# W2's block sums and split halves, made once and read back from DRAM, in a Strassen feed-forward kernel

## The chip, the cores and the metric

The kernel runs on one core of one Trainium2 chip. The metric is device time in microseconds (us), the median of several executions; smaller is better. The core's engines work side by side, each through its own queue in order: TensorE (PE in the profile; PEld is its weight load), VectorE (DVE), ScalarE (ACT), GpSimd (POOL) and SyncE (SP), which here only issues DMAs.

## The reference

Sliding-window attention with four sink tokens is followed by a Fourier mixing layer and a feed-forward block. The part that matters here is the end:

```python
u = x + mixed                               # x: attention output, 4 x 768 tokens x 512
mu = np.mean(u, axis=-1, keepdims=True)
var = np.mean((u - mu) ** 2, axis=-1, keepdims=True)
un = (u - mu) / np.sqrt(var + 1e-06)
ch = np.maximum(un @ w_ch1, 0.0) @ w_ch2    # w_ch1: 512 x 2048, w_ch2: 2048 x 512
return (u + ch).astype(np.float32)
```

All data is float32. TensorE multiplies in a rounded float32 (fp32r), so each operand is kept as a rounded high part and a low part, the rest, and a product is three matmuls: high x high, high x low, low x high.

## The kernel before

**Stages.** Attention and the Fourier mixing of the four batches come first; their code is not touched. The 3072 tokens are then taken through the feed-forward block in six groups of 512. Group 0 runs in a plain form while the weights are still being converted (`convert`, L595 and around), with W2 multiplied as it is. Groups 1 to 5 use a Strassen form of the second matmul; they are one loop (`for g in range(1, len(groups))`, L1391 on) that writes out the order of every engine's work by hand (`manual_schedule`), so each engine does its work exactly in the order of the code.

**A step.** Inside a group the loop over `q` runs eight times; this text calls one pass a step. A step handles 256 of the 2048 hidden columns, as two chunks of 128. `ch1` (matmuls on L629) multiplies the first chunk: 12 matmuls of 512 columns into one PSUM bank, `h0`. ScalarE's relu (L1396) moves it to the SBUF tile `r4`. Then TensorE does the first half of the products of the step before (`slot(prev, slice(0, 7))`, L1292, 21 matmuls of 256 columns), then `ch1` of the second chunk, whose relu is L1413, then the other half of the products (`slot(prev, slice(7, 14))`, 21 more). So TensorE alternates 12 + 21 + 12 + 21 matmuls a step. Because both `ch1` of a step write the same bank, the next `ch1` has to wait until the relu has emptied it; and that relu has to wait until VectorE has read the old contents of `r4`.

**The Strassen operands.** The left ones come from the hidden activations: `first_h`, `second_h` and `third_h` make four sums on VectorE (L1252, L1258, L1260, L1261) and split seven blocks into halves, the high one a ScalarE copy (L1247), the low one a VectorE subtraction (L1248): per step two of 256 columns, one of 512, one of 768. The right ones come from W2: `w_sums` makes four sums of 256 columns (L1272 to L1275) and `split_w` splits seven blocks in five pieces, the high halves on ScalarE (L1283), the low ones (L1284) on GpSimd, except for two pieces a step that VectorE does in the last group. W2 is the same for every group, but these sums and halves are made anew in each of the 40 steps, since only one set of them has room: the tiles `WC` (in the profile `w_ring`, `w2t`) are overwritten as soon as the products of the step before have read them.

**Work laid between.** `prepare(g + 1)` normalizes the next group's tokens in small pieces, taken by `next(steps, None)`: statistics (L507, L508), an inverse root by fourteen tiny operations (L514 to L523), the normalization (L531), sixteen 32 x 32-block transposes for each token block (`turn_blocks`, L1154), and the split of the result into `un_slots` or `un_last` (L541 ScalarE, L546 VectorE). Before, each step takes three pieces after its first half, one ahead of `third_h` and two behind it, so all is done by the seventh step. At the start of a group the seven accumulators of the group before are added into `u` (`finish_a`, `finish_b`, `finish_c`, L1314, VectorE), then three additions of SBUF to SBUF follow on GpSimd (`finish_d`, also L1314), and SP stores the result (L1349). `reload` (L1148) brings blocks of the other batches from DRAM into the freed places.

## Time and profile before

| | |
|---|---|
| median of 3 runs | 848.51 us (848.25 to 849.68) |
| profiled execution, its own time | 850.29 us |
| its span, first to last instruction | 848.5 us |
| VectorE busy | 714.5 us (84%) |
| ScalarE busy | 409.2 us (48%) |
| GpSimd busy | 543.2 us (64%) |
| bytes moved by DMA | 57.85 MB |

Engines overlap, so the shares add to more than the span. The five Strassen groups begin at 337.8, 437.4, 542.3, 645.8 and 750.7 us of the span, by the start of each group's first relu (L1396). A row of the trace gives start, duration, engine, line, operation and, in brackets, how long the engine had been idle before and for whom it waited. A row of a group gives busy time and mean duration in ns, and one of a single line minimum, median and maximum in ns. PEclk, in a row of windows, is the clock that TensorE was granted, 1.00 being full speed.

### The profile page before, as it was taken

To read this page: it belongs to the slowest core of one execution; us is meant where nothing else is said; L and a number is where in the kernel's file an instruction comes from. 1 tells how busy PE (TensorE), PEld (TensorE's weight loads), DVE (VectorE), ACT (ScalarE), POOL (GpSimd) and SP (SyncE) were. 2 spreads that over 40 slices of the span, in tenths; PEclk is the share of its full clock that TensorE was granted. 3 is DMA by queue.
4 is the path that set the end of the run, shared out by engine and by line. 5 is a ranking of instruction groups with operands and counts; after the bars stand their busy time and mean duration, and the time that the engine had idled before them with its cause. 6 is when DMAs were issued, how large, how long until landed. Compare 5 with 4: busy or idle time off the path is not lost.

```text
span 848.5 us, 14292 instructions
## 1 busy us (share of the span) xinstructions
PE 766.2 (90%) x4899; PEld 641.7 (76%) x4899; DVE 714.5 (84%) x1636; ACT 409.2 (48%) x1053; POOL 543.2 (64%) x644
## 2 busy tenths in 40 slices
PE   7989989989899999898897979979789788899994
PEld 5667767767788787787796867968679677799993
DVE  6786687897999995898889988899889997898765
ACT  5776665766332233353453434534445344455551
POOL 3465484585654454566596765968669585687762
PEclk9999999999989999989999989989999998999998
DMA  9835236333134560200000020000200000000001
GB/s 322 254 101 172 61 83 210 91 114 102 48 124 150 198 215 10 100 1 1 0 1 25 1 75 1 1 25 3 74 1 1 26 25 1 2 1 26 25 2 55
DMA packets 41827, 57.85 MB, mean 68 GB/s; under 512 B 2796, under 2 KB 27500, under 8 KB 41360
## 3 DMA queue, kind: packets, MB, share of 16 engines
q1 hardware_dynamic: 41456, 53.07, 19.7%
q0 software_dynamic: 288, 3.76, 1.1%
q8 instruction: 41, 0.67, 0.3%
q14 instruction: 42, 0.34, 0.1%
HBM read 47.37 MB, written 9.45 MB: 67 GB/s over the span
## 4 chain that ended last, share of the span: by engine, by line
PE 59%; DVE 28%; issue 6%; ACT 4%; POOL 2%; DMA 1%; SPq 0%; ACTq 0%; DVEq 0%; POOLq 0%
PE h L629 23%; PE p L1292 12%; DVE unf L1154 6%; PE o L1130 5%; DVE h_sums L1248 5%; PE xt L799 4%; PE s L712 4%; PE za L387 2%; PE pt L761 2%; DVE sums L1260 2%; DVE u L1314 1%; PE zb L387 1%; DVE sums L1258 1%; DVE f L344 1%; DVE un L531 1%
## 5 line engine op out<-in xcount | busy, mean ns | idle before, releaser
L1247 ACT CAST h_sums<-sums 128x256 fp32r<-128x256 f32 (+2 forms) x160 | 90.7, 567 | 185.1 <-DVE sums L1261 113.0
L1248 DVE TENSOR_TENSOR h_sums<-sums,h_sums 128x256 fp32r<-128x256 f32 (+2 forms) x160 | 137.8, 869 | 15.3 <-ACT h_sums L1247 9.9
L1292 PE MATMUL p<-w_ring,h_sums 128*128 128x256 f32 x960 | 136.3, 284 | 14.0 <-DVE h_sums L1248 8.8
L1292 PEld LDWEIGHTS p<-w_ring,h_sums 128*128 128x128 f32 x960 | 126.6, 191 | 18.7 <-DVE h_sums L1248 9.9
L1284 POOL TENSOR_TENSOR w2t<-sums,w2t 128x256 fp32r<-128x256 f32 x72 | 59.6, 828 | 112.2 <-ACT w2t L1283 111.8
L629 PE MATMUL h<-un_slots,w 128*128 128x512 f32 x396 | 108.6, 428 | 16.4 <-ACT sums L1396 16.2
L629 PE MATMUL h<-un_last,w 128*128 128x512 f32 x396 | 104.2, 415 | 18.1 <-ACT sums L1396 14.7
L1292 PE MATMUL p<-w2t,h_sums 128*128 128x256 f32 x720 | 112.5, 283 | 0.0
L629 PEld LDWEIGHTS h<-un_slots,w 128*128 128x128 f32 x396 | 80.5, 208 | 34.9 <-ACT sums L1396 17.4
L629 PEld LDWEIGHTS h<-un_last,w 128*128 128x128 f32 x396 | 77.5, 202 | 35.5 <-ACT sums L1396 16.1
L1292 PEld LDWEIGHTS p<-w2t,h_sums 128*128 128x128 f32 x720 | 101.0, 192 | 3.5
L736 ACT ACTIVATE sm<-sm,mx 128x132 f32<-128x132 f32 x192 | 75.9, 399 | 14.4 <-DVE mx L730 14.4
L1154 DVE STREAM_TRANSPOSE unf<-un 32x128 f32<-32x128 f32 x256 | 77.5, 303 | 4.2
L712 PE MATMUL s<-ring,q 64*128 64x260 f32 x320 | 55.6, 430 | 7.9 <-DVE mx L730 7.8
L1284 POOL TENSOR_TENSOR w_ring<-sums,w_ring 128x512 fp32r<-128x512 f32 x32 | 46.0, 1437 | 12.4 <-ACT w_ring L1283 11.7
L1284 POOL TENSOR_TENSOR w_ring<-w2r,w_ring 128x512 fp32r<-128x512 f32 x40 | 53.2, 1330 | 0.5 <-ACT w_ring L1283 0.5
L1258 DVE TENSOR_TENSOR sums<-sums 128x256 f32<-128x256 f32 x40 | 30.6, 766 | 26.7 <-ACT sums L1413 26.4
L747 POOL CAST sk<-sm 128x32 fp32r<-128x32 f32 x48 | 11.7, 244 | 64.6 <-ACT sm L736 64.6
L1284 POOL TENSOR_TENSOR w2t<-w2r,w2t 128x256 fp32r<-128x256 f32 x40 | 37.5, 938 | 20.0 <-ACT w2t L1283 20.0
L730 DVE CUSTOM_DVE_ANT_0 sm<-s,mask 128x132 f32<-128x132 f32 x192 | 47.5, 284 | 3.3 <-PE s L710 1.4
L718 DVE COPY_PREDICATED s<-older,s 128x256 f32<-128x256 uint8 x80 | 33.7, 422 | 16.7 <-PE s L712 16.4
L1413 ACT ACTIVATE sums<-h 128x512 f32<-128x512 f32 x40 | 23.8, 596 | 40.5 <-PE h L629 40.3
(235 smaller groups left out, 1770.0 us busy)
## 6 DMA issues: line engine op xcount, KB each, us to landing
raw<-in_moe_w_ch_dram SPq DMA_DIRECT2D x32, 512.0 KB, 3.3
ldv<-in_v_dram SPq DMA_DIRECT2D x28, 256.0 KB, 2.8
ring<-in_qk_dram SPq DMA_DIRECT2D x24, 264.0 KB, 5.0
out_dram<-u SPq DMA_DIRECT2D x24, 256.0 KB, 2.3
q<-in_qk_dram SPq DMA_DIRECT2D x20, 256.0 KB, 4.6
cst<-in_dft_dram POOLq DMA_DIRECT2D x1, 3348.0 KB, 12.7
ud<-us SPq DMA_DIRECT2D x12, 256.0 KB, 2.1
u<-ud SPq DMA_DIRECT2D x2, 1024.0 KB, 5.1
```

The source lines that it names most:

```text
L629: T.matmul(ps[:, :tb], a[:, cs], x[:, :, cc, :], start=n == 0, stop=n == 3 * NCC - 1)
L712: T.matmul(ps[:, j, :P + W], st["q", g][rows, hp, :], keys(g, 2 * hp + j), start=True, stop=True)
L730: V.tensor_tensor_reduce(sm[:, h % 4], ps[:, j, P:P + W], mask[min(qi, 3)], -SCALE, 3.0e38, ALU.add, ALU.min, accum_out=mx[:, 0, h:h + 1])
L736: A.activation(sm[:, h % 4], sm[:, h % 4], AF.Exp, bias=mx[:, 0, h:h + 1], scale=-1.0, accum_out=mx[:, 1, h:h + 1])
L799: T.matmul(ps[D * j:D * j + D, p, :], st["v", kb(g) - i][:, h, :], a[:, h % 4, :], start=i == 0, stop=i == n - 1)
L1130: T.matmul(po[i], a[:, ts_], x, start=f == 0 and n == 0, stop=f == NF - 1 and n == 2)
L1154: V.transpose(unf[32 * q:32 * q + 32, :, r], un[r].rearrange("p (c q j) -> p c q j", c=NCC, q=4)[:, :, q])
L1247: A.copy(hc_hi[:, left(a, n)], src)
L1248: V.tensor_tensor(hc_lo[:, left(a, n)], src, f32(hc_hi[:, left(a, n)]), op=ALU.subtract)
L1258: V.tensor_tensor(hs4[:, 1], r4[:, 0, 1], r4[:, 1, 1], op=ALU.add)
L1284: eng.tensor_tensor(lo, src, f32(hi), op=ALU.subtract)
L1292: T.matmul(acc[i][:, 2 * P * tp:2 * P * tp + 2 * P], x, w, start=q == 0 and tp == 0 and n == 0, stop=q == NF // 2 - 1 and n == 2, skip_gro ...
```

## The change

In group 1 the four sums and the low halves of W2's pieces are made on VectorE, and each finished piece is stored to a DRAM tile of its step (`w_dram`, `w2s` in the order below). In groups 2 to 5 `w_sums` and `split_w` are gone: five loads per step (`load_w2`, on SP's queue) bring both halves of each piece straight into the tiles. The three additions of `finish_d` move from GpSimd to VectorE; those of the last group's ending (`finish_last`) stay. The next group's blocks are, while group 1 runs, transposed by TensorE in the bank `h0` (`un_turn`), in the middle of the first half of the products; in groups 2 to 4 VectorE goes on transposing. The pieces of `prepare` are spread by two tables over all eight steps, `second_h` makes its sums before its split, `reload` comes two steps later, and group 0's outputs are finished in two portions.

```diff
+PREP_A = (0, 1, 1, 1, 1, 1, 1, 1), (0, 2, 2, 3, 3, 3, 3, 2)
+PREP_B = (1, 1, 1, 0, 0, 0, 0, 0), (1, 2, 2, 2, 2, 2, 2, 1)
-RELOAD_AT = 4
+RELOAD_AT = 6
+PARTS_W = (0, 0, 2, 0), (1, 0, 1, 2), (1, 1, 1, 3), (2, 0, 2, 4), (3, 0, 1, 6)
+    w_dram = [dpool.tile([P, 2, len(LEFT) * 2 * P], F32, name=f"w2s{q}") for q in range(NF // 2)]
...
                     un_make(b, blk, u)
                     yield
+                    if g == 2:
+                        turns.append((b, blk, unT, i))
+                        while turns:
+                            yield
+                        continue
...
-                split_h(r4[:, 1].rearrange("p t w -> p (t w)"), 2, 2)
                 V.tensor_tensor(hs4[:, 2], hs4[:, 1], r4[:, 0, 0], op=ALU.subtract)
                 V.tensor_tensor(hs4[:, 3], r4[:, 1, 0], hs4[:, 2], op=ALU.subtract)
+                split_h(r4[:, 1].rearrange("p t w -> p (t w)"), 2, 2)
...
-                G.tensor_tensor(t3, b22, b12, op=ALU.subtract)
+                V.tensor_tensor(t3, b22, b12, op=ALU.subtract)
...
+            def load_w2(q, i):
+
+                c, k, n, at_ = PARTS_W[i]
+                nc.sync.dma_start(f32(WC[c][:, :, 2 * P * k:2 * P * (k + n)]), w_dram[q][:, :, 2 * P * at_:2 * P * (at_ + n)])
...
                 A.copy(hi, src)
-                eng.tensor_tensor(lo, src, f32(hi), op=ALU.subtract)
+                V.tensor_tensor(lo, src, f32(hi), op=ALU.subtract)
+                nc.sync.dma_start(w_dram[q][:, :, 2 * P * at_:2 * P * (at_ + n)], f32(t))
...
-                    add(G, x, state["u2"])
+                    add(V, x, state["u2"])
...
-                        slot(prev, slice(0, 7))
+                        slot(prev, slice(0, 3))
+                        turned = turns.pop() if turns else None
+                        if turned:
+                            un_turn(*turned[:2], state["h"].tile([P, 512], F32, tag="h0", name=f"unt_{g + 1}_{turned[3]}"))
+                            un_hi(*turned)
+                            un_lo(*turned)
+                        slot(prev, slice(3, 7))
                         first_h()
...
+                            if prev[0] == 1 and prev[2]:
+                                split_w(prev[2], 3)
+                                split_w(prev[2], 4)
...
-                            w_sums(q)
-                            split_w(q, 1)
-                            split_w(q, 0)
-                        for _ in range(3):
+                            if g == 1:
+                                w_sums(q)
+                            else:
+                                load_w2(q, 1)
+                                load_w2(q, 0)
...
+                        for _ in range(PREP_A[g > 1][q]):
                             next(steps, None)
...
                         second_h()
+                        if g > 1:
+                            for i in range(2, 5):
+                                load_w2(q, i)
+                        elif q:
+                            for i in (1, 0, 2):
+                                split_w(q, i)
...
-                        for _ in range(2):
+                        for _ in range(PREP_B[g > 1][q]):
                             next(steps, None)
```

The first place is VectorE in the middle of group 1, one step (`sums` are the operand sums, `un`/`unf` the normalized block and its transpose). Before:

```order
L1252 TENSOR_TENSOR sums_4176<-sums_4175 128x256
L1248 TENSOR_TENSOR h_sums<-sums_4175,h_sums 128x256
L1248 TENSOR_TENSOR h_sums<-sums_4176,h_sums 128x256
L531 TENSOR_SCALAR un_3_4549<-u_65,stat_2_4259 128x512
L1154 STREAM_TRANSPOSE unf_1_4551<-un_3_4549 32x4x32 x8
L1258 TENSOR_TENSOR sums_4176<-sums_4175 128x256
L1248 TENSOR_TENSOR h_sums<-sums_4175,h_sums 128x512
L1260 TENSOR_TENSOR sums_4176<-sums_4176,sums_4175 128x256
L1261 TENSOR_TENSOR sums_4176<-sums_4175,sums_4176 128x256
L1154 STREAM_TRANSPOSE unf_1_4551<-un_3_4549 32x4x32 x4
L1248 TENSOR_TENSOR h_sums<-sums_4176,h_sums 128x768
L1154 STREAM_TRANSPOSE unf_1_4551<-un_3_4549 32x4x32 x4
```

And of the change, from the split of the previous step's last two pieces on, to the split of the next ones:

```order
L1298 TENSOR_TENSOR w_ring<-sums_4184,w_ring 128x512
L1298 TENSOR_TENSOR w2t_3956<-w2r_3554,w2t_3956 128x256
L1280 TENSOR_TENSOR sums_4184<-w2r_3722 128x256
L1281 TENSOR_TENSOR sums_4184<-w2r_3722 128x256
L1282 TENSOR_TENSOR sums_4184<-w2r_3722,sums_4184 128x256
L1283 TENSOR_TENSOR sums_4184<-w2r_3722,sums_4184 128x256
L534 TENSOR_SCALAR un_3_4656<-u_65,stat_2_4265 128x512
L1266 TENSOR_TENSOR sums_4183<-sums_4182 128x256
L1267 TENSOR_TENSOR sums_4183<-sums_4183,sums_4182 128x256
L1268 TENSOR_TENSOR sums_4183<-sums_4182,sums_4183 128x256
L1256 TENSOR_TENSOR h_sums<-sums_4182,h_sums 128x512
L1298 TENSOR_TENSOR w2t_3304<-sums_4184,w2t_3304 128x256
```

Nine operations on W2 stand in VectorE's row where none stood, and the sixteen transposes of a block are gone from it.

The second place is VectorE in group 2, from the sums of the second half of its second step (`u_1` is the part of the accumulators that three blocks share). Before:

```order
L1258 TENSOR_TENSOR sums_4176<-sums_4175 128x256
L1248 TENSOR_TENSOR h_sums<-sums_4175,h_sums 128x512
L1260 TENSOR_TENSOR sums_4176<-sums_4176,sums_4175 128x256
L1261 TENSOR_TENSOR sums_4176<-sums_4175,sums_4176 128x256
L519 SCALAR_TENSOR_TENSOR stat_0_5153<-stat_0_5153 128x4
```

And of the change:

```order
L1266 TENSOR_TENSOR sums_4183<-sums_4182 128x256
L1267 TENSOR_TENSOR sums_4183<-sums_4183,sums_4182 128x256
L1268 TENSOR_TENSOR sums_4183<-sums_4182,sums_4183 128x256
L1256 TENSOR_TENSOR h_sums<-sums_4182,h_sums 128x512
L1329 TENSOR_TENSOR u_64<-u_64,u_1_5084 128x2x256
L517 TENSOR_SCALAR stat_0_5143<-stat_0_5143 128x4
```

One of GpSimd's three additions a group has come in, and the inverse root begins here instead of in the half before.

The third place is SP's queue in group 2 (`w2s` is the DRAM copy, `ud` a batch kept in DRAM). Before, these rows follow each other, the last already of group 3:

```order
L1349 DMA out_dram<-u_64 128x512 x2
L1349 DMA out_dram<-u_65 128x512 x2
L1148 DMA u_64<-ud_66 128x1024
L1148 DMA u_65<-ud_67 128x1024
L1349 DMA out_dram<-u_65 128x512 x4
```

With the change, from the same stores on:

```order
L1364 DMA out_dram<-u_64 128x512 x2
L1364 DMA out_dram<-u_65 128x512 x2
L1288 DMA w2t_3304<-w2s_73 128x2x256
L1288 DMA w_ring<-w2s_73 128x2x512
L1288 DMA w2t_3304<-w2s_73 128x2x256
L1288 DMA w_ring<-w2s_73 128x2x512
L1288 DMA w2t_3956<-w2s_73 128x2x256
L1288 DMA w2t_3304<-w2s_74 128x2x256
```

Five loads a step, 256, 512, 256, 512 and 256 KB, stand in one queue with the stores and reloads.

More of the change, by code (lines that the diff above doesn't have):

```diff
@@ L603, in convert @@
                     if which:
-                        state["w2t", f] = d
+                        state["w2t", f] = state["ring"][:, 2 * i:2 * i + 2]
                 elif which:
                     if f == 2:
-                        state["w2t", f] = [pool.tile([P, 512], F32R, name=f"w2t{f}_{j}") for j in range(2)]
-                    d = state["w2t", f % 3]
+                        state["w2t", f] = pool.tile([P, 2, 512], F32R, name="w2t2")
+                    d = [state["w2t", f % 3][:, j] for j in range(2)]
                 elif W_FOLD <= f < W_FOLD + NHALF:
@@ L1130, in ch2, with finish @@
                         T.matmul(po[i], a[:, ts_], x, start=f == 0 and n == 0, stop=f == NF - 1 and n == 2)
-            def finish(g, po, us):
-                for i, (b, blk) in enumerate(groups[g]):
+            def finish(g, po, us, part):
+                for i, (b, blk) in list(enumerate(groups[g]))[part]:
                     V.tensor_tensor(us[i], po[i], us[i], op=ALU.add)
@@ L1239, in run @@
             hc_hi, hc_lo = hc[0][:, 0], hc[0][:, 1]
-            WC = [state["w2t", i] for i in (1, 2, 0)] + [[hc[1][:, i] for i in range(2)]]
+            WC = [state["w2t", i] for i in (1, 2, 0)] + [hc[1]]
             def left(a, n=1):
@@ L1289, in product @@
                 hi, lo = (t[:, 2 * P * a + P * tp:2 * P * a + P * tp + P] for t in (hc_hi, hc_lo))
-                w_hi, w_lo = (t[:, 2 * P * k:2 * P * k + 2 * P] for t in WC[c])
+                w_hi, w_lo = (WC[c][:, j, 2 * P * k:2 * P * k + 2 * P] for j in range(2))
                 for n, (x, w) in enumerate(((hi, w_hi), (hi, w_lo), (lo, w_hi))):
@@ L1384, in finish_last @@
                         nc.sync.dma_start(out[b, blk], u_of(b, blk))
-            prev, late = None, iter(())
+            prev, late, turns = None, iter(()), []
             with tc.manual_schedule():
@@ L1398, in run @@
                             ch2(NF - 1, hs[NF - 1], po, slice(0, 2))
[L1399 to L1401 removed]
+                        slot(prev, slice(0, 3))
[5 more added lines that the diff above has]
+                        slot(prev, slice(3, 7))
+                        first_h()
+                        if prev is not None:
+                            if prev[0] == 1 and prev[2]:
+                                split_w(prev[2], 3)
+                                split_w(prev[2], 4)
+                            if prev[2] == NF // 2 - 1:
+                                finish_a(*prev[:2])
+                            if g == 1:
[3 more added lines that the diff above has]
+                                load_w2(q, 0)
+                        if q == 1 and g == 1:
+                            finish(0, po, us, slice(1, 4))
+                        elif q == 1:
                             finish_c(*old)
                             late = finish_d(old[0])
[L1404 to L1410 removed]
+                        for _ in range(PREP_A[g > 1][q]):
                             next(steps, None)
@@ L1417, in run @@
                         second_h()
+                        if g > 1:
[4 more added lines that the diff above has]
+                                split_w(q, i)
                         if prev is None:
                             split_w(0, 3)
-                            finish(0, po, us)
-                        else:
-                            for i in range(2, 5):
-                                split_w(q, i, V if g == len(groups) - 1 and i < 4 else G)
-                            if prev[2] == NF // 2 - 1:
-                                finish_b(*prev[:2])
-                                old = prev[:2]
+                            finish(0, po, us, slice(0, 1))
+                        elif prev[2] == NF // 2 - 1:
+                            finish_b(*prev[:2])
+                            old = prev[:2]
                         if q == 0:
@@ L1432, in run @@
                             reload(g - 1)
-                        if q == 0:
-                            if g + 1 < len(groups):
-                                steps = prepare(g + 1)
+                        if q == 0 and g + 1 < len(groups):
+                            steps = prepare(g + 1)
                         next(steps, None)
                         third_h()
-                        for _ in range(2):
+                        for _ in range(PREP_B[g > 1][q]):
                             next(steps, None)
```

20 lines of the change are left out of this document (8 added, 12 removed).

## The prediction

> **What bounds the kernel now.** The page first. Its first part gives TensorE's busy share, and the windows by group (each from the first relu of a group to that of the next, the last row being the stretch of group 5 that follows) say where the rest goes.
>
> ```profile
> PE 766.2 (90%) x4899; PEld 641.7 (76%) x4899; DVE 714.5 (84%) x1636; ACT 409.2 (48%) x1053; POOL 543.2 (64%) x644
> ```
>
> ```profile
> 337.80:437.40 99.60, 88.82 (x510) 78.20 (x509) 85.94 (x161) 44.19 (x89) 63.75 (x66) 0.95 0.06 22
> 437.40:542.30 104.90, 91.84 (x530) 80.89 (x530) 93.95 (x167) 46.42 (x94) 75.97 (x76) 0.93 0.06 21
> 542.30:645.80 103.50, 89.93 (x530) 79.56 (x530) 93.58 (x167) 46.56 (x95) 76.04 (x76) 0.95 0.06 21
> 645.80:750.70 104.90, 91.77 (x530) 80.78 (x529) 93.93 (x167) 46.45 (x95) 75.95 (x76) 0.93 0.03 11
> ...
> 750.70:830.00 79.30, 79.30 (x500) 71.80 (x500) 61.14 (x85) 43.14 (x87) 57.53 (x57) 1.00 0.04 14
> ```
>
> TensorE is busy for 90% of the span and VectorE for 84%: two candidates. In the windows the columns are length, then busy time of PE, PEld, DVE, ACT and POOL, clock, DMA share, GB/s. Groups 2 to 4 take 104 us each with VectorE busy for 94 of them. Group 5, the same matmuls with no next group to prepare, runs with TensorE never idle at full clock. So the matmuls alone aren't the limit of groups 2 to 4. How fast they could go is read from the timeline, by the relus of first chunks (L1396): the first of group 1 and the one after it, the first of group 2, and three of group 5.
>
> ```profile
> 337.79 0.60 ACT L1396 ACTIVATE sums<-h 128x512 f32<-128x512 f32 x1 [3.30 <-PE h L629]
> 346.38 0.59 ACT L1396 ACTIVATE sums<-h 128x512 f32<-128x512 f32 x1
> 437.40 0.59 ACT L1396 ACTIVATE sums<-h 128x512 f32<-128x512 f32 x1
> 760.04 0.60 ACT L1396 ACTIVATE sums<-h 128x512 f32<-128x512 f32 x1 [0.37 <-PE h L629]
> 770.56 0.60 ACT L1396 ACTIVATE sums<-h 128x512 f32<-128x512 f32 x1 [1.56 <-PE h L629]
> 823.26 0.60 ACT L1396 ACTIVATE sums<-h 128x512 f32<-128x512 f32 x1 [1.60 <-PE h L629]
> ```
>
> From 770.56 to 823.26 lie five steps: **10.54 us a step**. From 437.40 to 760.04 lie 25 steps in 322.64 us, where TensorE alone would need 25 x 10.54 = 263.5: 59.1 us are lost. Group 1 took 99.6.
>
> Who is waited for stands in the waits from 345 us on; behind it a long wait with its price, and the same twelve matmuls undisturbed:
>
> ```profile
> PEld h L629 <- ACT sums L1396: 36.9, 15, 5.2
> PE p L1292 <- DVE u L1314: 5.2, 3, 1.7
> ```
>
> ```profile
> 494.53 5.49 PE L629 MATMUL h<-un_slots,w 128*128 128x512 f32 x12 [4.52 <-ACT sums L1396]
> ...
> 772.87 2.91 PE L629 MATMUL h<-un_last,w 128*128 128x512 f32 x12
> ```
>
> The relu is named, but ScalarE is busy for 46 of 104 us; its relu is late because `r4` is still being read by VectorE, which does its queue in order. And a wait of 4.52 us costs 5.49 - 2.91 = 2.6 us more, as the matmuls behind it run slower. VectorE's lateness is the bound of groups 2 to 4.
>
> **Why VectorE is late.** By line and form in groups 2 to 4 (busy us, mean ns), and the shortest of such operations:
>
> ```profile
> L1154 DVE STREAM_TRANSPOSE unf<-un 32x128 f32<-32x128 f32 x192 | 58.1, 303 | 3.0
> L1248 DVE TENSOR_TENSOR h_sums<-sums,h_sums 128x512 fp32r<-128x512 f32 x24 | 28.4, 1182 | 1.1 <-ACT h_sums L1247 0.7
> L1248 DVE TENSOR_TENSOR h_sums<-sums,h_sums 128x768 fp32r<-128x768 f32 x24 | 26.6, 1108 | 6.4 <-ACT h_sums L1247 3.4 <-PE p L1292 2.7
> L1260 DVE TENSOR_TENSOR sums<-sums,sums 128x256 f32<-128x256 f32 x24 | 26.3, 1095 | 0.0
> L1248 DVE TENSOR_TENSOR h_sums<-sums,h_sums 128x256 fp32r<-128x256 f32 x48 | 25.6, 545 | 3.0 <-ACT h_sums L1247 2.7
> L1261 DVE TENSOR_TENSOR sums<-sums,sums 128x256 f32<-128x256 f32 x24 | 23.9, 998 | 0.8
> L1258 DVE TENSOR_TENSOR sums<-sums 128x256 f32<-128x256 f32 x24 | 20.9, 871 | 7.1 <-ACT sums L1413 7.0
> L1252 DVE TENSOR_TENSOR sums<-sums 128x256 f32<-128x256 f32 x24 | 14.9, 620 | 3.7 <-ACT sums L1396 3.5
> ```
>
> ```profile
> L1260 DVE TENSOR_TENSOR sums<-sums,sums x40: 411/957/1510, 343.8 to 830.4; 128x256 f32<-128x256 f32 x40
> ...
> L1284 DVE TENSOR_TENSOR w_ring<-sums,w_ring x8: 680/956/1264, 759.6 to 831.5; 128x512 fp32r<-128x512 f32 x8
> ...
> 477.98 0.96 DVE L1248 TENSOR_TENSOR h_sums<-sums,h_sums 128x768 fp32r<-128x768 f32 x1
> ```
>
> One operation of one size takes 0.41 or 1.51 us. The timeline shows why:
>
> ```profile
> 778.81 0.74 POOL L1284 TENSOR_TENSOR w2t<-w2r,w2t 128x256 fp32r<-128x256 f32 x1 [2.06 <-ACT w2t L1283]
> 778.84 1.26 DVE L1284 TENSOR_TENSOR w_ring<-sums,w_ring 128x512 fp32r<-128x512 f32 x1
> 779.51 1.74 POOL L1314 TENSOR_TENSOR u<-u,u 128x512 f32<-128x512 f32 x1
> 780.03 2.04 DVE L1248 TENSOR_TENSOR h_sums<-sums,h_sums 128x768 fp32r<-128x768 f32 x1
> ```
>
> The first VectorE row ends at 780.10, 0.55 us after GpSimd's first row; the second at 782.07, 0.82 us after GpSimd's second. Each does nearly all its 0.68 or 0.96 us behind a GpSimd operation. I read it as: a VectorE operation with two SBUF inputs stands still while GpSimd is in one.
>
> **The change, part by part: groups 2 to 4.** GpSimd falls silent, so I take the short durations. Saved over three groups: 24 x (1182 - 680) + 24 x (1108 - 960) + 24 x (1095 - 411) + 48 x (545 - 411) + 24 x (998 - 411) + 24 x (871 - 411) + 24 x (620 - 411) ns = 68.6 us, 22.9 a group. The moved additions of `finish_d` cost 3 x 0.68 = 2.0. VectorE goes from 93.8 to about 73 us a group, under TensorE's 8 x 10.54 = 84.3. The spread of `prepare` over eight steps keeps the steps alike: the fullest, the second, holds 4.1 us of activation work (six operations of 0.41, one of 0.68, one of 0.96), five additions of 0.68 and five pieces of `prepare` (two of statistics, twelve tiny operations: some 4 us, an estimate), near 11.5 us, and the next hold less than 10.5. TensorE asks for a sum half a step (5.3 us) after its relu at the earliest, which covers that. So 263.5 us for the 25 steps. Of the wait on L1314, 5.2 us, which belongs to the accumulators, I keep half: 266.1. **Gain 56.5 us**; between 59.1 (all of it) and about half, 28, if late work is only halved.
>
> ScalarE loses five copies a step, off the path. Group 5 is dense already: nothing.
>
> **Loads.** Per step 256 + 512 + 256 + 512 + 256 KB, 1.84 MB in 10.54 us: 174 GB/s. Here a load waits for the products that read the old piece, and behind it on SP stand the later loads and group stores. Durations by size, and the best rate of the trace, its first slice:
>
> ```profile
> raw<-in_moe_w_ch_dram SPq DMA_DIRECT2D x32, 512.0 KB, 3.3
> ldv<-in_v_dram SPq DMA_DIRECT2D x28, 256.0 KB, 2.8
> ```
>
> ```profile
> 0.00:21.20 21.20, 16.69 (x120) 11.84 (x120) 14.43 (x80) 11.76 (x44) 7.43 (x25) 1.00 0.98 322
> ```
>
> Each piece is read once in a step of 10.54 us, within at most 18 neighbouring matmuls of 256 columns, some 2.2 us, so some 8 us lie between its last reader and its next one. The second piece of `w2t` is read in both halves, with a `ch1` of 2.9 us between, which leaves some 7 us. A load of 2.8 or 3.3 us has 4 us to spare. I cost the loads at nothing, hidden by the 10.5 us step; with that cover gone they cost what the first rival says. Issuing takes SP some 0.33 us each, which nobody waits for.
>
> The Trainium skill (page "DMA: Bandwidth & Descriptors", section "Measured (HBM→SBUF, 128 partitions, SWDGE, issued from GpSimd)") speaks against these loads: batch to 1 MiB or more for three quarters of the peak rate. By the fit in its section "Anatomy of one DMA — SWDGE (gpsimd) path", 2.0 us fixed plus bytes at 436 GB/s, five loads one by one would take an estimated 14 us a step, more than TensorE's. Both sections measured another queue than SP's. The trace's 322 GB/s, more than three times what one transfer of 256 KB in 2.8 us gives, shows that transfers overlap, so I side with the row.
>
> **Group 1.** VectorE now does, per step, 4.1 us for activations and 4.2 for W2 (seven operations of 0.41, two of 0.68), plus, in the fullest steps, a normalization and its split, 1.4: 9.7, under 10.5. Without the sixteen transposes a block (16 x 0.303 = 4.8 us) there is room. The blocks turn on TensorE instead:
>
> ```profile
> 320.19 0.60 PE L537 MATMUL unt<-ident,un 128*128 128x128 f32 x4
> 320.55 3.02 PE L629 MATMUL h<-un_slots,w 128*128 128x512 f32 x12
> ```
>
> The next matmul follows 0.36 us after; but the bank has to be read by ScalarE and VectorE before `ch1` may write it, beside only twelve products: 0.6 us a block, four blocks, 2.4. The second and third steps, which also finish group 0 and take the statistics, hold more than 10.5 us on VectorE, with little slack, since W2's pieces are due right behind their split: 1.5. First step as before, 346.38 - 337.79 = 8.6. So 8.6 + 7 x 10.54 + 2.4 + 1.5 = 86.3 against 99.6: **gain 13.3**, between 15.8 (TensorE alone, with 0.36 a block) and 0. The stores of these steps hold up nobody: a piece is written again ten us later.
>
> **Ahead of group 1** the first sums and low halves, 4 x 0.41 + 0.68 + 3 x 0.41 = 3.6 us, come to VectorE in this window:
>
> ```profile
> 300.00:345.00 45.00, 43.88 (x199) 35.65 (x198) 30.91 (x49) 16.65 (x30) 21.33 (x20) 1.00 0.28 93
> ```
>
> It is busy for 31 of 45 us there, TensorE for 44; the cost lies between 0 and 3.6, I take **1.0**.
>
> **Sum.** The span 848.5 stands 1.8 under that execution's own 850.29, and the runs' median is 848.51, so what changes is taken off 848.5: 848.5 - 56.5 - 13.3 + 1.0 = 779.7, said as 780.
>
> **The rivals.** *Loads one after another* (slower). If SP's loads ran in turn, a step would need 3 x 2.8 + 2 x 3.3 = 15.0 us in groups 2 to 5: 32 x 15.0 = 480 us, where 437.40 to 823.26 plus one step took 396.4. The end: 848.5 + 83.6 - 13.3 + 1.0 = 920. It beats the gain of group 1 from (396.4 + 12.3) / 32 = 12.8 us a step on. Against it: the rate of the first slice. 4%.
>
> *GpSimd is not what stretches VectorE* (slower). Then its 94 us a group stay, plus 2, and group 1 gets 8 x 4.2 us longer, less 64 x 0.303: near +14; with +1 and some 2 a group at most, 848.5 + 14 + 1 + 6 = 870. Against it: the 0.41 us that the same operation can take, and the four rows of the timeline. 2%.
>
> *VectorE is still late at the full steps*, half of the loss stays, with its slow matmuls: 848.5 - 28 - 7 + 1 = 815. For it: a late relu costs 7.1 us with the slow matmuls behind it, and `prepare`'s transposes still stand among the sums. Against it: 73 of 84 us. 14%. What lies between it and the forecast is the likelier part of it.
>
> *The same matmuls without any stall:* 848.5 - 59.1 - 15.8 = 773.6; this is the low end of the forecast's own case.
>
> **The numbers.** Forecast (773 to 793) 78%, still late (793 to 815) 14%, slower by the two mechanisms 6%, loads or waits that just eat the gain 2%. The range goes from 772 to 808, into the third rival. A difference within 0.2% (1.7 us) can't be told from none: faster 0.92, same 0.02, slower 0.06.
>
> **What would show it.** Relus L1396 of groups 2 to 4 10.5 us apart; the four sums' means at 0.41 to 0.45 us, VectorE near 73 us a group; GpSimd silent from 340 us to the ending; loads landing within 4 us of their issue; TensorE's clock at 1.00 for 500 us. I am wrong if products wait for DMA, if a relu still waits for VectorE, or if group 1 stays over 90 us.

## The result, and the profile after

| | before | after |
|---|---|---|
| median | 848.38 us (848.23 to 849.68, 4 runs) | 777.55 us (777.47 to 779.1, 4 runs) |
| ratio of after to before | | 0.9166, 95% interval 0.915 to 0.9182 |
| profiled execution, its own time | 850.29 us | 777.47 us |
| its span | 848.5 us | 775.7 us |
| bytes moved by DMA | 57.85 MB | 131.23 MB |

The kernel became 8.3% faster, 70.8 us by the medians, where the forecast was 780, a fall of 68.8. In the profiled executions it is 72.8; that execution of before lay 1.9 us above its median. In one of the four runs of `e3_before_spread` below the granted clock was 0.838, where the other three had 0.966 to 0.978, and the time 858.84 us; that entry's numbers are those of the other three.

The page's first part for the changed kernel, its lines numbered anew (the relus are now L1411 and L1441, `ch1` L632, the products L1307, the four sums L1260 and L1266 to L1268, the splits L1256, the additions to `u` L1329, the loads L1288):

```profile
PE 741.1 (96%) x4915; PEld 626.8 (81%) x4915; DVE 601.3 (78%) x1640; ACT 344.1 (44%) x893; POOL 186.4 (24%) x288
```

Its windows by group (length, busy time of PE, PEld, DVE, ACT and POOL, clock, DMA share, GB/s), and the relus with which group 1 and its second step, group 2, the second step of group 5 and the last step begin:

```profile
337.65:422.80 85.15, 85.02 (x517) 75.53 (x516) 68.77 (x160) 43.23 (x87) 0.00 (x0) 1.00 0.45 166
422.80:507.00 84.20, 84.20 (x530) 76.19 (x529) 68.65 (x172) 31.28 (x55) 0.00 (x0) 1.00 0.67 215
507.00:591.30 84.30, 84.30 (x531) 76.31 (x531) 67.72 (x170) 30.57 (x54) 0.00 (x0) 1.00 0.64 200
591.30:675.50 84.20, 84.20 (x530) 76.21 (x529) 67.73 (x170) 30.46 (x53) 0.00 (x0) 1.00 0.61 187
675.50:775.70 100.20, 86.75 (x558) 78.88 (x557) 47.14 (x90) 28.81 (x50) 3.97 (x3) 0.96 0.54 172
```

```profile
337.65 0.60 ACT L1411 ACTIVATE sums<-h 128x512 f32<-128x512 f32 x1 [3.30 <-PE h L632]
345.81 0.60 ACT L1411 ACTIVATE sums<-h 128x512 f32<-128x512 f32 x1 [1.24 <-PE h L632]
...
422.76 0.60 ACT L1411 ACTIVATE sums<-h 128x512 f32<-128x512 f32 x1 [2.03 <-PE h L632]
...
686.04 0.60 ACT L1411 ACTIVATE sums<-h 128x512 f32<-128x512 f32 x1 [2.03 <-PE h L632]
...
749.26 0.60 ACT L1411 ACTIVATE sums<-h 128x512 f32<-128x512 f32 x1 [2.03 <-PE h L632]
```

In groups 2 to 4 TensorE is now busy for the whole of each window at a clock of 1.00. The 25 steps from 422.76 to 686.04 take 263.28 us, 10.53 each: the 59.1 us that were lost there are gone to the last one. VectorE works 68 of 84 us, GpSimd not at all.

The waits from 335 us on, of which three rows matter:

```profile
POOL u L1329 <- ACT u L1382: 431.3, 1, 431.3
...
PE p L1307 <- DMA w_ring<-w2s: 1.7, 1, 1.7
...
PEld h L632 <- DVE un_slots L549: 0.7, 4, 0.2
```

The wait of `ch1`'s weight load for the relu, 36.9 us before, has no row any more. What is left of TensorE's waits in 440 us is one of 1.7 us for a load, at which its weight load stands still too, and some tenths. The first row says that GpSimd sat idle for 431 us, up to the ending.

The groups by line and form, in groups 2 to 4 (busy us, mean ns of one):

```profile
L1256 DVE TENSOR_TENSOR h_sums<-sums,h_sums 128x512 fp32r<-128x512 f32 x24 | 16.4, 685 | 0.0
L1268 DVE TENSOR_TENSOR sums<-sums,sums 128x256 f32<-128x256 f32 x24 | 10.2, 425 | 0.8
L1267 DVE TENSOR_TENSOR sums<-sums,sums 128x256 f32<-128x256 f32 x24 | 10.2, 425 | 0.8
...
L534 DVE TENSOR_SCALAR un<-u,stat 128x512 f32<-128x512 f32 x12 | 6.5, 543 | 0.1
```

The split of 512 columns took 1182 ns before, the two sums 1095 and 998.

By stretch, before against after: up to the first relu of group 1, 337.79 and 337.65 (-0.1); group 1, 99.61 and 85.11 (-14.5); 25 steps, 322.64 and 263.28 (-59.4); from the second step of group 5 to the end, 848.5 - 760.04 = 88.5 and 89.7 (+1.2). Together -72.8.

That last +1.2 was not foreseen. The timeline of the last step shows it:

```profile
756.30 0.52 SPq L1288 DMA_DIRECT2D w_ring<-w2s  x1
...
758.99 0.88 PE L1307 MATMUL p<-w2t,h_sums 128*128 128x256 f32 x6
...
761.61 1.67 PE L1307 MATMUL p<-w_ring,h_sums 128*128 128x256 f32 x12 [1.74 <-DMA w_ring<-w2s]
```

In the ending the products of the last step follow one another with no `ch1` between, so the load issued at 756.30 is wanted 3.6 us later and lands after 5.

### The profile page after: what moved, and what is told of

It is laid out like the page before. It is cut to its first block, busy times and chain, and to the rows that moved or that the text cites. A ratio compares the mean times of both kernels' runs of the same rounds, so it can differ in the third digit from the quotient of the medians.

```text
span 775.7 us, 14193 instructions
## 1 busy us (share of the span) xinstructions
PE 741.1 (96%) x4915; PEld 626.8 (81%) x4915; DVE 601.3 (78%) x1640; ACT 344.1 (44%) x893; POOL 186.4 (24%) x288
## 2 busy tenths in 40 slices
DMA packets 96224, 131.23 MB, mean 169 GB/s; under 512 B 5996, under 2 KB 61420, under 8 KB 95760
## 4 chain that ended last, share of the span: by engine, by line
PE 80%; DVE 13%; ACT 2%; issue 2%; DMA 1%; POOL 1%; SPq 0%; ACTq 0%; DVEq 0%; POOLq 0%
PE h L632 32%; PE p L1307 25%; PE o L1133 4%; PE xt L802 4%; PE s L715 4%; PE za L390 2%; PE pt L764 2%; PE zb L390 1%; DVE f L347 1%; DVE sm L733 1%; PE zr L390 1%; DVE s L721 1%; PE x L814 1%; DVE gl L363 1%; DMA vt<-in_v_sink_dram 1%
## 5 line engine op out<-in xcount | busy, mean ns | idle before, releaser
L1307 PE MATMUL p<-w_ring,h_sums 128*128 128x256 f32 x960 | 134.5, 283 | 1.9 <-DMA w_ring<-w2s 1.7
L1307 PEld LDWEIGHTS p<-w_ring,h_sums 128*128 128x128 f32 x960 | 126.0, 191 | 5.4 <-issue 1.9
L1307 PE MATMUL p<-w2t,h_sums 128*128 128x256 f32 x720 | 112.9, 283 | 0.0
L1256 DVE TENSOR_TENSOR h_sums<-sums,h_sums 128x256 fp32r<-128x256 f32 (+2 forms) x160 | 99.5, 622 | 15.1 <-ACT h_sums L1255 14.0
L1329 POOL TENSOR_TENSOR u<-u,u 128x512 f32<-128x512 f32 x2 | 2.8, 1376 | 434.9 <-ACT u L1382 431.3
L1307 PEld LDWEIGHTS p<-w2t,h_sums 128*128 128x128 f32 x720 | 100.3, 191 | 3.1
L632 PE MATMUL h<-un_last,w 128*128 128x512 f32 x396 | 96.5, 392 | 0.0
L632 PE MATMUL h<-un_slots,w 128*128 128x512 f32 x396 | 96.3, 391 | 0.0
L632 PEld LDWEIGHTS h<-un_slots,w 128*128 128x128 f32 x396 | 72.7, 188 | 14.1
L632 PEld LDWEIGHTS h<-un_last,w 128*128 128x128 f32 x396 | 72.2, 188 | 14.5 <-DVE un_slots L549 0.7
L1441 ACT ACTIVATE sums<-h 128x512 f32<-128x512 f32 x40 | 23.9, 598 | 98.3 <-PE h L632 98.3
L1157 DVE STREAM_TRANSPOSE unf<-un 32x128 f32<-32x128 f32 x192 | 58.1, 302 | 2.8
L1266 DVE TENSOR_TENSOR sums<-sums 128x256 f32<-128x256 f32 x40 | 16.9, 421 | 49.2 <-ACT sums L1441 48.9
L1411 ACT ACTIVATE sums<-h 128x512 f32<-128x512 f32 x40 | 24.0, 599 | 66.8 <-PE h L632 66.8
L715 PEld LDWEIGHTS s<-ring,q 64*128 64x128 f32 x320 | 24.8, 184 | 22.1 <-issue 10.3
L802 PE MATMUL xt<-ptl,ldv 128*64 128x128 f32 x384 | 39.0, 285 | 0.0
L739 ACT ACTIVATION_READ_ACCUMULATOR sm<-sm,mx 128x1 f32 x192 | 36.7, 191 | 0.0
```

The source lines that it names most:

```text
L632: T.matmul(ps[:, :tb], a[:, cs], x[:, :, cc, :], start=n == 0, stop=n == 3 * NCC - 1)
L715: T.matmul(ps[:, j, :P + W], st["q", g][rows, hp, :], keys(g, 2 * hp + j), start=True, stop=True)
L739: A.activation(sm[:, h % 4], sm[:, h % 4], AF.Exp, bias=mx[:, 0, h:h + 1], scale=-1.0, accum_out=mx[:, 1, h:h + 1])
L802: T.matmul(ps[D * j:D * j + D, p, :], st["v", kb(g) - i][:, h, :], a[:, h % 4, :], start=i == 0, stop=i == n - 1)
L1157: V.transpose(unf[32 * q:32 * q + 32, :, r], un[r].rearrange("p (c q j) -> p c q j", c=NCC, q=4)[:, :, q])
L1256: V.tensor_tensor(hc_lo[:, left(a, n)], src, f32(hc_hi[:, left(a, n)]), op=ALU.subtract)
```

## The experiments

In the diffs, `-` and `+` stand against the kernel that each entry names. Line numbers of the kernels differ by a few.

**GpSimd put back beside VectorE, with nothing for it to do: `e1_gp_reads`** (against the changed kernel; `wt4` is idle in groups 2 to 5):

```diff
+            tick = wl.tile([P, 1], F32, name="tick")
...
+            def busy(part):
+                G.tensor_copy(tick, hs4[:, 0, 0:1])
+                for n in part:
+                    t = wt4[:, 0:n]
+                    G.tensor_tensor(t, t, wt4[:, 4 - n:4], op=ALU.subtract)
...
                                 load_w2(q, 0)
+                                busy((1, 1, 1, 1, 1, 2))
...
                             for i in range(2, 5):
                                 load_w2(q, i)
+                            busy((1, 2, 1))
```

> The changed kernel, and GpSimd is given nine subtractions a step in groups 2 to 5 (seven of 256 columns, two of 512, as many as it had before) on a tile that nobody reads there; nothing waits for them but a one-column copy that paces them. My theory (GpSimd's own SBUF work stretches VectorE's two-input operations): the four sums' means go from 0.42 back to 0.6 to 1.1 us, VectorE to 88 us a group or more, groups 2 to 4 to 92 us or more each, the time to 800 to 840 us. Rival (the gain is that VectorE, ScalarE and TensorE no longer wait for results of GpSimd): nothing waits here, so the sums stay near 0.42 us and the time within 2 us of 777.5.

Measured: 829.4 us (828.38 to 830.42, 2 runs), ratio to before 0.9774 (0.9699 to 0.985). Its window of group 3 and its forms of groups 2 to 4:

```profile
526.20:626.40 100.20, 90.52 (x530) 79.86 (x529) 92.40 (x171) 29.96 (x53) 72.30 (x89) 0.95 0.53 169
```

```profile
L1291 POOL TENSOR_TENSOR sums<-sums 128x256 f32<-128x256 f32 x167 | 135.7, 812 | 9.3
...
L1269 DVE TENSOR_TENSOR sums<-sums,sums 128x256 f32<-128x256 f32 x24 | 32.2, 1342 | 0.8
...
L1337 DVE TENSOR_TENSOR u<-u,p 128x512 f32<-128x512 f32 x27 | 16.8, 675 | 0.0
...
L1337 DVE TENSOR_TENSOR u<-u,u 128x512 f32<-128x512 f32 x9 | 9.4, 1040 | 0.0
```

The same VectorE instructions take 92.4 us a group instead of 67.7, and the groups 100 us instead of 84. Nobody reads what GpSimd makes, and no row of the waits in groups 2 to 4 names GpSimd as what another engine waited for. So its SBUF work alone gives back 52 of the 71 us. The last two rows tell which operations are hit: the additions with both inputs in SBUF (`u<-u,u`) take 1040 ns, 684 in the changed kernel; those with one input in PSUM (`u<-u,p`, the accumulators) take 675 ns, 682 there.

**The same places, filled without reading: `e2_gp_memset`**

```diff
-                    G.tensor_tensor(t, t, wt4[:, 4 - n:4], op=ALU.subtract)
+                    G.memset(wt4[:, 0:n], 0.0)
```

> As the run with the subtractions, but GpSimd fills the same regions with zeros, so it writes SBUF and reads none, but for the one-column copy. If any work of GpSimd stretches VectorE, the sums' means rise as there, in proportion to the time GpSimd is busy. If only operations that read SBUF do, they stay at 0.42 to 0.45 us and the time at 777 to 780 us. The Trainium skill (page "SBUF — State Buffer", section "SBUF: two separate sides") says the second: VectorE's operations with two SBUF inputs clash only with a GpSimd operation that reads SBUF.

Measured: 778.12 us (777.64 to 778.59, 2 runs), ratio 0.917 (0.91 to 0.924). Its window of group 2, and its forms:

```profile
424.10:508.30 84.20, 84.20 (x530) 76.20 (x529) 68.77 (x172) 31.34 (x55) 28.82 (x88) 1.00 0.66 214
```

```profile
L1290 POOL MEMSET sums<- 128x256 f32 x168 | 52.9, 315 | 6.9
...
L534 DVE TENSOR_SCALAR un<-u,stat 128x512 f32<-128x512 f32 x12 | 7.1, 592 | 0.1
```

GpSimd is busy for a third of the group here, less than half as long as in e1, since a memset is shorter (315 ns against 812). The four sums keep their 425 ns, but that proves little: the nine memsets of a step begin behind the first sum and are over before the other three begin, but for three cases in 72. What does run beside them is the second split of 256 columns in each step. One step, first here and then in e1 (the `sums` that GpSimd writes are the idle `wt4`):

```profile
499.31 2.38 POOL L1290 MEMSET sums<- 128x256 f32 x6
499.57 0.43 DVE L1257 TENSOR_TENSOR h_sums<-sums,h_sums 128x256 fp32r<-128x256 f32 x1 [0.24 <-ACT h_sums L1256]
...
501.75 1.27 POOL L1290 MEMSET sums<- 128x256 f32 x3
...
503.70 0.43 DVE L1267 TENSOR_TENSOR sums<-sums 128x256 f32<-128x256 f32 x1 [3.71 <-ACT sums L1449]
```

```profile
553.61 2.44 POOL L1291 TENSOR_TENSOR sums<-sums 128x256 f32<-128x256 f32 x3
...
553.80 0.83 DVE L1257 TENSOR_TENSOR h_sums<-sums,h_sums 128x256 fp32r<-128x256 f32 x1 [0.19 <-ACT h_sums L1256]
```

All 24 such splits of groups 2 to 4 take 0.42 to 0.43 us inside the memsets, the same as the 24 first splits that meet none, where a weaker form of the same clash would have shown something; inside the subtractions of e1 they take 0.78 to 0.96. It is GpSimd's reading that VectorE's two-input operations wait for, not its being busy, nor its writing.

The Trainium skill (page "SBUF — State Buffer", section "SBUF: two separate sides") states this as a lock: a VectorE operation with two SBUF inputs is shut out only by a GpSimd operation that reads SBUF, and whichever starts first holds the ports for its whole instruction. On the first half the traces agree, 0.83 us beside reads and 0.43 beside memsets; the second half no run here tests by itself.

**Only the spread of `prepare`, in the kernel before: `e3_before_spread`**

```diff
-PREP_AT, PREP_M = 1, 3
+PREP_A = 0, 2, 2, 3, 3, 3, 3, 2
+PREP_B = 1, 2, 2, 2, 2, 2, 2, 1
...
-                        for _ in range(3):
+                        for _ in range(PREP_A[q]):
...
-                        for _ in range(2):
+                        for _ in range(PREP_B[q]):
```

> The kernel before, W2 on GpSimd as it was, with the pieces of the next group's preparation spread over all eight steps by the change's second row of each table, in all groups. My theory: VectorE keeps its 94 us a group, so groups 2 to 4 can come down to some 95 us each but not to 84; 815 to 838 us. Rival (the even spread of the preparation is what made TensorE dense): 770 to 795 us.

Measured: 837.26 us (829.37 to 838.68, 3 runs), ratio 0.9829 (0.9731 to 0.9927). The window of its group 3:

```profile
536.10:637.70 101.60, 90.25 (x530) 79.71 (x529) 90.38 (x168) 46.28 (x94) 74.56 (x76) 0.95 0.06 22
```

An even load shortens the whole time by some 1.7% (0.7 to 2.7) and does no more: VectorE still needs 90 us and GpSimd 75.

**GpSimd silent, but no copy in DRAM: `e5_after_vector_w2`** (the changed kernel, where VectorE and ScalarE make W2's sums and halves in every step):

```diff
-                nc.sync.dma_start(w_dram[q][:, :, 2 * P * at_:2 * P * (at_ + n)], f32(t))
...
-                            if prev[0] == 1 and prev[2]:
+                            if prev[2] or prev[0] > 1:
...
-                            if g == 1:
-                                w_sums(q)
-                            else:
-                                load_w2(q, 1)
-                                load_w2(q, 0)
+                            w_sums(q)
...
-                        if g > 1:
-                            for i in range(2, 5):
-                                load_w2(q, i)
-                        elif q:
+                        if q or g > 1:
...
+                for i in (3, 4):
+                    split_w(prev[2], i)
```

> The changed kernel with no DRAM copy: VectorE and ScalarE make W2's sums and halves in every step of every group, GpSimd stays silent. My theory (VectorE's load must stay under TensorE's 84 us a group): VectorE gets 8 x 4.2 = 34 us a group more, near 102, and groups 2 to 4 take 102 us or more each: 777.5 + 3 x 18 = 830, up to 845 with slow matmuls. Rival (silencing GpSimd is enough, the copy buys nothing): 777 to 785 us.

Measured: 843.0 us (840.04 to 845.12, 8 runs), ratio 0.9932 (0.9903 to 0.9961). Its window of group 3, and two rows of its waits over groups 2 to 4:

```profile
529.20:634.20 105.00, 93.35 (x530) 82.22 (x529) 97.40 (x243) 45.92 (x94) 0.00 (x0) 0.92 0.06 21
```

```profile
PEld h L632 <- ACT sums L1436: 15.9, 6, 3.4
...
PEld p L1306 <- DVE w_ring L1298: 14.3, 13, 2.4
```

No operation is stretched, but VectorE does 243 of them instead of 170. Silence alone is worth almost nothing, 0.7%, when VectorE inherits the work: the gain needs both, no reads of GpSimd beside VectorE and the work made once.

**`prepare`'s pieces early again, in the changed kernel: `e4_after_early_prep`**

```diff
-                        for _ in range(PREP_A[g > 1][q]):
+                        for _ in range(3 if g > 1 else PREP_A[0][q]):
...
-                        for _ in range(PREP_B[g > 1][q]):
+                        for _ in range(2 if g > 1 else PREP_B[0][q]):
```

> The changed kernel, with prepare's pieces laid in groups 2 to 4 as in the kernel before: three after a step's first half, then one and one, so that all are done by the seventh step; everything else as changed. My theory: the unstretched operations are what brought the gain, and VectorE's fullest step (some 11.5 us) is still covered by the 5.3 us that TensorE gives each relu. So groups 2 to 4 stay at 84 to 85.5 us each and the time at 777 to 781. Rival: the spread was needed for the dense groups too; then each early step runs over by 1 us or more and late relus with slow matmuls come back, 3 us or more a group, 787 or more, with waits of PEld for the relu in the groups' first five steps.

Measured: 779.17 us (778.18 to 783.49, 4 runs), ratio 0.9211 (0.9178 to 0.9243). Group 3:

```profile
507.10:591.80 84.70, 84.51 (x530) 76.26 (x529) 68.06 (x170) 30.26 (x53) 0.00 (x0) 1.00 0.63 199
```

Half a microsecond a group. With unstretched operations even five pieces in one step are covered but for that: the relus of a group's fourth to sixth steps come 11.1, 12.1 and 9.0 us after the one before instead of 10.5, so what is late is nearly made up.

**The turns given back to VectorE in group 1: `e7_turn_on_vector`**

```diff
-                    if g == 2:
+                    if g == 99:
                         turns.append((b, blk, unT, i))
...
-                        for _ in range(PREP_A[g > 1][q]):
+                        for _ in range(PREP_A[1][q]):
...
-                        for _ in range(PREP_B[g > 1][q]):
+                        for _ in range(PREP_B[1][q]):
```

> The changed kernel, but in group 1 VectorE transposes the next group's blocks (64 transposes of 0.303 us, 19.4 us) and the pieces of prepare follow the same table as in groups 2 to 4; TensorE transposes nothing there. VectorE's 68.8 us of group 1 become about 88 us, over the 84.3 us of TensorE's eight steps. My theory: group 1 becomes bound by VectorE, 89 to 95 us instead of 85.1, and the time is 781 to 788. Rival: the turns on TensorE only moved idle time, since they cost TensorE some 0.6 us a block themselves; then group 1 stays within 2 us and the time at 775 to 779.5.

Measured: 789.8 us (789.44 to 790.72, 4 runs), ratio 0.9323 (0.9303 to 0.9342). Group 1, and its waits there:

```profile
338.30:436.50 98.20, 86.66 (x500) 75.22 (x499) 88.29 (x224) 43.30 (x86) 0.00 (x0) 0.98 0.38 142
```

```profile
PEld p L1307 <- DVE w_ring L1298: 7.1, 7, 3.8
...
PEld h L632 <- ACT sums L1441: 5.8, 2, 3.5
```

VectorE's 88 us came as computed, and the group takes 98.2, more than the 89 to 95 expected: I had priced VectorE's busy time and left out that TensorE waits for W2's pieces, which stand in the same queue, as well as for the relus. Of the 14.5 us that group 1 gained, 13.1 rest on the turns and on the table of pieces that goes with them.

**Loads taken away: `e8_no_loads`**

```diff
 def load_w2(q, i):
-                nc.sync.dma_start(f32(WC[c][:, :, 2 * P * k:2 * P * (k + n)]), w_dram[q][:, :, 2 * P * at_:2 * P * (at_ + n)])
+                pass
```

> The changed kernel with the loads of W2's pieces left out in groups 2 to 5: every step there multiplies by the pieces that the last step of group 1 left in the tiles. What is left out: 160 loads, 59 MB. My theory: the loads are hidden but for the wait of 1.7 us for the piece of the last step, so 775.5 to 777. Rival: the loads still cost time in ways that show in no wait on them (issuing on SP, stores held up behind them, SBUF writes beside the engines); then the time falls below 774.

Measured: 776.71 us (775.19 to 780.74, 4 runs), ratio 0.9181 (0.9147 to 0.9214). In its trace the 25 steps run from 422.67 to 685.96, 263.29 us, as with the loads. Its span is 773.5, and the difference lies behind the last step's first relu: 24.32 us to the end instead of 26.44. All 59 MB cost nothing outside the last step.

**Each load twice into one place: `e6_double_loads`**

```diff
+                for _ in range(2):
                     nc.sync.dma_start(f32(WC[c][:, :, 2 * P * k:2 * P * (k + n)]), w_dram[q][:, :, 2 * P * at_:2 * P * (at_ + n)])
```

> The changed kernel with each of the five loads a step issued twice in a row into the same place: 3.67 MB a step of 10.53 us, 349 GB/s, where the best slice of the profile of before moved 322 GB/s. My theory (a single load has some 4 us to spare, but the step's bytes are about half of what the queues can move): the doubled loads cannot be hidden, a step needs at least 3.67 MB / 322 GB/s = 11.4 us, 32 steps gain 28 us or more: 805 to 880, with waits of PE for w_ring or w2t. Rival: transfers have far more room than I think and the time stays within 5 us of 777.5; then the cover of the loads is no limit near this size.

Measured: 1189.45 us (1189.22 to 1195.33, 5 runs), ratio 1.4034 (1.4006 to 1.4061). SP's own row shows why it went so far beyond 880 (a run of two issues, from the start of the first to the end of the second), beside SP's longest wait in the window of group 2, and that window:

```profile
600.54 5.03 SPq L1289 DMA_DIRECT2D w_ring<-w2s  x2
605.62 4.41 SPq L1289 DMA_DIRECT2D w2t<-w2s  x2
```

```profile
SPq L1289 <- DMA w2t<-w2s: 70.6, 22, 4.9
```

```profile
425.10:601.30 176.20, 113.29 (x528) 97.30 (x526) 69.72 (x172) 31.28 (x56) 0.00 (x0) 0.82 0.52 168
```

An issue takes 0.52 us; two take 4.4 to 5.0, and SP's row of waits names the load itself: the second was issued when the first, into the same place, had landed. Only 168 GB/s moved. It was no test of the rate, as I had meant it, but of something close to the rival in which loads run one after another: five such waits in a row make a step of 22 us in this window.

**A second load into another place: `e12_loads_elsewhere`** (the idle places of raw W2):

```diff
                 nc.sync.dma_start(f32(WC[c][:, :, 2 * P * k:2 * P * (k + n)]), w_dram[q][:, :, 2 * P * at_:2 * P * (at_ + n)])
+                nc.sync.dma_start(Wr[i].bitcast(F32)[:, :, 0:2 * P * n], w_dram[q][:, :, 2 * P * at_:2 * P * (at_ + n)])
```

> The changed kernel with a second load beside each of W2's loads, of the same bytes, into the places of raw W2, which nothing reads in groups 2 to 5; no two loads of a step write one place, so no second load waits for a first (in e6_double_loads each did, and they ran in turn). 3.67 MB a step of 10.53 us would be 349 GB/s. My theory: the queues move 322 GB/s at best, so a step takes at least 11.4 us: 32 steps, 28 us or more, 805 to 850, with waits of TensorE for w_ring or w2t. Rival: the cover is larger than I think, and the time stays under 785, with each load landing later (over 6 us) but still in time.

Measured: 787.06 us (785.97 to 790.4, 4 runs), ratio 0.9272 (0.9248 to 0.9297). Three issues in a row, less than a microsecond apart, the window of group 3, and the loads between 440 and 690 us with their median us to landing:

```profile
519.39 0.61 SPq L1289 DMA_DIRECT2D w2r<-w2s  x1
520.27 0.52 SPq L1288 DMA_DIRECT2D w_ring<-w2s  x1
520.83 1.00 SPq L1289 DMA_DIRECT2D w2r<-w2s  x1
```

```profile
513.20:597.80 84.60, 84.50 (x528) 75.82 (x527) 67.74 (x170) 30.53 (x54) 0.00 (x0) 1.00 1.04 370
```

```profile
w_ring<-w2s SPq DMA_DIRECT2D x47, 512.0 KB, 6.0
...
w2t<-w2s SPq DMA_DIRECT2D x71, 256.0 KB, 5.8
```

My theory fell: nearly all steps stay at 10.5 us with twice the bytes, at 370 GB/s, above the 322 that I had taken for the most. The window's DMA share, 1.04, leaves no idle time, so there can't be much room beyond; no run tried more. The rival's "under 785" is missed by 2 us too. From the first relu of group 1 to the end it is 788.7 - 341.59 = 447.1 us, against 438.1 in the changed kernel: some 9 us in all, in five single steps of 11.5 to 12 us, with waits of TensorE for `w_ring`, and a longer ending, where a doubled load cost 28 or more by my account.

**The last step's piece made instead of loaded, and the ending reordered: `e9_last_piece_made`, `e10_last_piece_and_end`, beside `e11_after_again`.** e9 against the changed kernel:

```diff
-            def split_w(q, i):
+            def split_w(q, i, keep=True):
...
-                nc.sync.dma_start(w_dram[q][:, :, 2 * P * at_:2 * P * (at_ + n)], f32(t))
+                if keep:
+                    nc.sync.dma_start(w_dram[q][:, :, 2 * P * at_:2 * P * (at_ + n)], f32(t))
...
                                 load_w2(q, 0)
+                                if g == len(groups) - 1 and q == NF // 2 - 1:
+                                    w_sums(q)
...
-                                load_w2(q, i)
+                                if i == 3 and g == len(groups) - 1 and q == NF // 2 - 1:
+                                    split_w(q, i, False)
+                                else:
+                                    load_w2(q, i)
```

e10 against e9:

```diff
                 add(V, x22, p5)
-                add(V, x22, s2)
                 add(V, x12, p5)
                 add(V, x12, p3)
-                for t in (1, 0):
+                add(V, x22, s2)
+                for t in (0, 1):
```

> The changed kernel, but in the last step of the last group VectorE makes W2's four sums and the low half of the fourth piece again, and ScalarE its high half, so that piece is not loaded. My theory: the wait of 1.74 us of TensorE for that load is what the ending lost (1.2 us more than before the change); without it the time falls by 1.2 to 1.7 us, to 775.8 to 776.4 beside 777.5 of the changed kernel on the same chip. Rival: the ending is bound by VectorE's additions and the output stores; then it stays within 0.5 us of the changed kernel.

> The kernel of e9, and in the ending the addition of s2 to x22 (1.77 us beside a GpSimd addition, where 0.69 us alone) comes behind the two additions from PSUM into x12, with the stores of the first two blocks first. My theory: that addition no longer meets GpSimd's two in SBUF, so VectorE ends some 1 us sooner and the time is 0.5 to 1.2 us below e9's: 774.8 to 775.8. Rival: GpSimd's own additions run later too, or the stores set the end, and the time is within 0.4 us of e9's.

> The changed kernel itself, beside e9 and e10 on the same chip: 777.0 to 778.2.

Measured on one chip: e9 775.46 us (774.37 to 776.36), ratio 0.9138 (0.9117 to 0.9159); e10 777.99 (774.67 to 779.75), ratio 0.9159 (0.9132 to 0.9186); e11 777.17 (775.1 to 778.96), ratio 0.9161 (0.9136 to 0.9185); five runs each. These intervals overlap; the traces say more. From the last step's first relu to the end: e11 775.5 - 750.25 = 25.25 us, the changed kernel's first trace 26.44, e9 773.6 - 749.85 = 23.75, e10 777.3 - 753.11 = 24.19. In e9 the twelve products that had waited follow at once:

```profile
759.59 0.88 PE L1308 MATMUL p<-w2t,h_sums 128*128 128x256 f32 x6
760.31 1.60 PE L1308 MATMUL p<-w_ring,h_sums 128*128 128x256 f32 x12
```

So e9 is 1.5 to 2.7 us better in the ending of these single traces, and the fastest of all kernels here by its median. In e10 the addition of `s2` to `x22` does go from 1.76 to 0.68 us, and VectorE ends 1.0 us sooner after those products, but the last store is issued at 771.3, 2.2 us behind VectorE's last addition at 769.1: the stores set the end, as its rival had it, and in all four traces the span ends some 5.5 us behind the last store's issue. Why the stores of e10 were issued so late is not shown. Its median is no evidence against the edit either, since its profiled execution came 3.4 us later to group 1 than e9's (341.60 against 338.21), in code that the two share.

## Why the prediction was right

**The bound and its cause.** VectorE's lateness bounded groups 2 to 4, and GpSimd's reading made VectorE late: shown by e1 and e2, where GpSimd's work is put back and nothing waits for it. The rival that GpSimd is not the cause falls with e1. What the prediction left unsaid is that silence isn't enough (e5).

**Groups 2 to 4: 266.1 forecast, 263.3 measured.** The mis-sized term is the kept half of the wait on the accumulators' additions: I kept 2.6 of 5.2 us, and nothing of it stayed. VectorE came to 68 us a group where I had 73, since the sum of rows left out others that were stretched too: `un`, 890 ns before and 543 after, its low half, 1036 and 686, and, the largest share, 36 tiny operations of the inverse root (L519, L521, L523), 412 to 548 ns before and 166 to 168 after. The low end of the forecast's case, no stall at all, is what these groups do.

**The spread of `prepare`** keeps steps alike, as said, but e4 shows that it is worth only 0.5 us a group once nothing is stretched; the 5.3 us before each sum is wanted do cover the fullest step.

**Group 1: 86.3 forecast, 85.1 measured.** Of the 1.2 us, the first step is 8.2 instead of 8.6; the second to fourth steps lose 0.5 together instead of 1.5; and the four steps with a turn take 0.7 more each instead of 0.6:

```profile
377.87 0.60 ACT L1411 ACTIVATE sums<-h 128x512 f32<-128x512 f32 x1 [2.08 <-PE h L632]
389.06 0.60 ACT L1411 ACTIVATE sums<-h 128x512 f32<-128x512 f32 x1 [1.73 <-PE h L632]
```

That is one step with a turn, 11.19 us. That the turns had to leave VectorE is shown by e7.

**Ahead of group 1: +1.0 forecast, -0.1 measured,** and neither can be told from nothing: the changed kernel and eight runs with the same code up to there (e2, e4 and e7 to e12) reach group 1 between 337.35 and 341.60 us. This term stays open.

**The loads: nothing forecast, and nothing measured but in the last step.** e8 shows it for the 25 steps. The sizes were off: the loads land after 4.3 and 3.2 us instead of 3.3 and 2.8, and an issue takes SP 0.52 us instead of 0.33. These are the loads by size, from 422.8 to 686 us:

```profile
w_ring<-w2s SPq DMA_DIRECT2D x50, 512.0 KB, 4.3
w2t<-w2s SPq DMA_DIRECT2D x75, 256.0 KB, 3.2
```

The 4 us to spare were enough, though the larger loads missed the sign "within 4 us of their issue", and e12 says that they hold, in all but a few steps, up to about 6 us of landing time. The rival of loads in turn falls: in e12 ten loads a step are issued without waiting for one another.

The Trainium skill's rule to batch to 1 MiB (page "DMA: Bandwidth & Descriptors", section "Measured (HBM→SBUF, 128 partitions, SWDGE, issued from GpSimd)") was measured on another queue and does not bind here: pieces of 256 and 512 KB, several under way at once, moved 370 GB/s in e12.

**What was missed** is the ending. "Group 5 is dense already: nothing" took group 5's steps for all of it, and the last step's products, with no `ch1` between, leave a load only 3.6 us. There products did wait for DMA, one of the prediction's signs of being wrong. It cost 1.2 us in the first trace and nothing in e11, where the wait was 0.9; without it the ending would have been shorter than before, 24.3 us (e8) against 848.5 - 823.26 = 25.2.

**VectorE still late** (815), the likeliest rival, fell: no relu waits for it any more.

**How close.** In the spans, 779.7 against 775.7, the forecast was 4.0 us too high, 2.8, 1.2 and 1.1 us in the terms above less the 1.2 of the ending. That the medians differ by only 2.2 is in part luck: the execution from which the forecast took its 848.5 was slower than the median of before.

## What to carry to other kernels

Where VectorE's operations of one size take several different times, look at what GpSimd reads in the same microseconds before moving any work: here that reading cost 52 us, with nobody waiting for GpSimd. What is the same in each pass is worth storing in DRAM if each load has a time of its own well above its landing time, counted at the end of the loop too, where the work that covers it stops. And moving work off a clashing engine pays only if the one that gets it has room: remove it first, then move what is left.

## What had not been expected of the hardware

A memset by GpSimd leaves VectorE's two-input operations as they are, 0.43 us for 256 columns, but the normalization `un`, with one tensor input, takes 0.74 us in the three of twelve cases of e2 that fell among memsets and 0.54 in the other nine. Loads of 256 and 512 KB from one queue reached 370 GB/s over a group of 84.6 us, with landing times of about 6 us instead of 3.2 and 4.3. In e6 SP held a second load into the place of one still under way until that had landed, and with it all that stood behind; the time rose by 412 us. Whether the chip asks for this wait or only the program is not shown. And what differs between the traced executions lies mostly ahead of the Strassen groups, the rest in the ending: in the traces of the changed kernel, e8, e9, e10 and e11 the 25 steps take 263.28 to 263.32 us, while group 1 begins up to 4 us apart.
